# A bank for each pair's small products, and left queries of two batches in one stage: linear attention and a maxout feed-forward on one core

## The chip, the cores and the metric

The kernel runs on one core of one Trainium2 chip. The metric is the device time of one execution in microseconds (us). Before the change the median of 3 runs is 717.27 us (717.15 to 717.32). Engines are named as the profile names them: PE (matmul), PEld (weight load of PE), DVE (vector), ACT (scalar), POOL and SP (whose queue issues the DMAs).

## The reference

Softmax over features for the queries, over positions for the keys, a linear attention, and then a maxout feed-forward on the rows of all heads side by side:

```python
batch, n_heads, seq, head_dim = (8, 8, 576, 64)
q_s = exp(q - max(q, -1)); q_s = q_s / (sum(q_s, -1) + 1e-09)
k_s = exp(k - max(k, 2));  k_s = k_s / (sum(k_s, 2) + 1e-09)
kv = np.einsum('bhsd,bhse->bhde', k_s, v)
attn = np.einsum('bhsd,bhde->bhse', q_s, kv)
x = attn.transpose(0, 2, 1, 3).reshape(4608, 512)
h = maximum(maximum(x @ w1, x @ w2), x @ w3)      # 512 -> 768
out = h @ w_out                                   # 768 -> 512
```

Queries, keys, values and the output are fp32, the weights fp64 in memory. The 576 positions of a batch are handled as 512 "main" rows and 64 "left" rows.

## The kernel before, in words

**Pairs.** Two heads of one batch are a pair (class `Pair`, L374); there are 8 x 4 = 32 of them, numbered n = 4b + g. A pair makes a 128x128 block-diagonal matrix of its two `kv` (L503 to L538, "bd"), and then its 128 rows of the transposed x: 512 main columns and 64 left columns (`x_steps`, L650). The pairs of batches 0 and 1 are "turned": keys and queries are loaded by rows and transposed on PE (L441, L464, L636; the left rows at L445, L466, L640). The query's exps are ten small ACT operations of 128x64 with their sums (L567) for the pairs in `Q_BY_ACT`, and a DVE or POOL subtraction, one exp and a DVE sum for the others (L572, L587, L589). The pairs of later batches use other paths (L475, L580 to L623) and start only when the step "turn" (L818) is reached: all weight slices are split, and all left products of batch 1 are there.

**Weights.** The weights lie in memory as fp64 and come in 24 slices of 512x128 or 128x512 (class `Slice`), each loaded by one DMA of 512 KB and split by ACT, DVE and POOL into a high and a low fp32r part (L342 to L370).

**Chunks.** A chunk is the 512 main rows of one batch; chunk 8 is the 64 left rows of all eight batches (the tile `left`). For each of 18 gates (3 weights x 6 column blocks) PE runs four groups of three fp32r matmuls (L693), one group for each pair's x; then ACT and DVE form the maximum (L702 to L712), and a second product (L732) makes the output.

**PSUM.** There are eight banks: four for the accumulators of gates and output (pool `pf`), three for pairs (`pa`), and one bank `ps` whose four quarters are handed out in turn to every small product: the left transposes of k (`kTl`), of its exps (`kel`) and of q (`qTl`), the `kv` product, and the left x product (L305, L306).

**Order of the work.** Nothing is ordered by the code's sequence. Every operation is a `Step` with a planned cost, its inputs, its rooms (buffers) and a rank. `Streams.run` (L142) simulates all engines and issues the step that can begin first; among those that can, the lowest rank goes first. The order of each engine's instructions that comes out is fixed in the program. The constants in L34 to L43 set the ranks: `AT` for the pairs of the first two batches, `FIRST` and `CHUNK` for the later ones, `SLICES_AT` and what follows for the weights, `GATES_AT` for the gates, and `FIRST_LOADS` for the first DMAs. The rooms in L302 limit what the planner may have open at once; `pf` is a queue whose order is written out beforehand (`in_pf`).

Of the kernel before, what the change touches and what calls it, by code (L numbers as in the profile page):

```python
# [42 lines left out]
Q_BY_ACT = (0, 1, 2, 3, 4, 5, 6)  # L43
# [36 lines left out]
class Streams:  # L80
# [115 lines left out]
def linear_attention_then_maxout_ffn(  # L196
# [26 lines left out]
    nc = tc.nc  # L223
# [22 lines left out]
    pa = ctx.enter_context(tc.tile_pool(name="pa", bufs=3, space=PSUM))  # L246
    ps = ctx.enter_context(tc.tile_pool(name="ps", bufs=1, space=PSUM))
# [16 lines left out]
    q0 = early.tile([P, H, 5, D], F32, name="q0")  # L264
    v0 = early.tile([P, H, 5, D], F32, name="v0")
    bdf = [start.tile([P, P], F32, name=f"bdf{i}", bufs=1) for i in range(2)]
    qbuf = [start.tile([P, 2, 5, D], F32, name=f"q1{i}", bufs=1) for i in range(2)]
# [14 lines left out]
    nc.gpsimd.memset(q0[LEFT:P, :, 4, :], 0.0)  # L282
    for i in range(2):
        nc.gpsimd.memset(bdf[i], 0.0)
    for i in range(2):
        nc.gpsimd.memset(qbuf[i][LEFT:P, :, 4, :], 0.0)
        nc.gpsimd.memset(vbuf[i][:, :, :, D:NV], 1.0)
        nc.gpsimd.memset(vbuf[i][LEFT:P, :, 4, :], 0.0)
# [13 lines left out]
    st = Streams({"pf": 4, "pa": 3, "ps": 4, "keT": 1, "hp": NJ, "tmp": 3, "ke": 2, "qe": 2, "qf": 1, "qt": 2, "tb": 1, "qT": 2, "qhl": 1}, {"pf": in_pf})  # L302
# [71 lines left out]
    class Pair:  # L374


        def __init__(self, b, g):
# [7 lines left out]
            else:  # L385
                self.kt, self.vt = kbuf[self.m], vbuf[self.m]
                if self.turned:
                    self.kt = self.kt.rearrange("p h s d -> p (h s d)").rearrange("p (s h d) -> p s h d", s=5, h=2)

        def ago(self, what, *u):  # L390

            return (what, self.n - 2, *u) if self.n >= 2 else None

# [15 lines left out]
        def v_load(self):  # L409
            if self.b:  # L410
                prev = self.ago("kv") if self.n >= NP + 2 else None
                for hh in range(2):
                    yield Step("S", 0.64, [prev], kb=200)
# [4 lines left out]
        def q_load(self):  # L418
            if self.b == 0:
                return  # L420
            if self.turned:
                prev = self.ago("qsub") if self.n >= NP + 2 else None
                self.qt = qbuf[self.m]
                yield Step("S", 0.64, [prev], kb=256)
                nc.sync.dma_start(out=self.qt[:, :, 0:4, :], in_=main_rows(q, self.b, self.hs))
                yield Step("S", 0.64, gives=("q", self.n), kb=50)
                nc.sync.dma_start(out=self.qt[0:LEFT, :, 4, :], in_=left_rows(q, self.b, self.hs))
# [6 lines left out]
        def k_turned(self):  # L434

            n, kt = self.n, self.kt
            rooms = [("pa", ("kT", n)), ("ps", ("kTl", n))]
            yield Step("T", 0.6, [("k", n)], take=rooms + [("keT", n)], gives=("ksub", n))
            kT = pa.tile([P, CH], F32, name="pa")
            for s in range(4):  # L440
# [3 lines left out]
            kTl = next(small)  # L444
            nc.tensor.transpose(  # L445
                out=kTl[:, :LEFT], in_=kt[:LEFT, 4].rearrange("p h d -> p (h d)"), identity=ident[:LEFT, :LEFT]
            )
            yield Step("V", dve_reduce(CH) + dve_reduce(LEFT) + 0.13)
            km = att.tile([P, 2], F32, name="km2", bufs=4)
            nc.vector.tensor_reduce(out=km[:, 0:1], in_=kT, op=ALU.max, axis=AX.X, negate=True)  # L450
            nc.vector.tensor_reduce(out=km[:, 1:2], in_=kTl[:, :LEFT], op=ALU.max, axis=AX.X, negate=True)
            nc.vector.tensor_tensor(out=km[:, 0:1], in0=km[:, 0:1], in1=km[:, 1:2], op=ALU.min)
            yield Step("A", act(CH) + act(LEFT) + 0.2, free=rooms)
            keT = start.tile([P, S], F32, name="keT", bufs=1)
            ks = self.ks = att.tile([P, 2], F32, name="ks", bufs=4)
            nc.scalar.activation(out=keT[:, :CH], in_=kT, func=AF.Exp, bias=km[:, 0:1], accum_out=ks[:, 0:1])  # L456
            nc.scalar.activation(
                out=keT[:, CH:], in_=kTl[:, :LEFT], func=AF.Exp, bias=km[:, 0:1], accum_out=ks[:, 1:2]
            )
            rooms = [("pa", ("ke", n)), ("ps", ("kel", n))]  # L460
            yield Step("T", 0.6, take=rooms + [("ke", n)], free=[("keT", n)])
            kep = pa.tile([P, CH], F32, name="pa")
            for s in range(4):
                nc.tensor.transpose(out=kep[:, s * P : (s + 1) * P], in_=keT[:, s * P : (s + 1) * P], identity=ident)  # L464
            kel = next(small)
            nc.tensor.transpose(out=kel[:LEFT, :], in_=keT[:, CH:], identity=ident)  # L466
            e = yield Step("AV", (act(CH) + act(P), dve(CH) + dve(P)), free=rooms)
            ke = self.ke = att.tile([P, 5, 2, D], F32, name="ke")
            for o, i in (
                (ke[:, 0:4].rearrange("p s h d -> p (s h d)"), kep),  # L470
                (ke[:LEFT, 4].rearrange("p h d -> p (h d)"), kel[:LEFT, :]),
            ):
                (nc.scalar.copy if e == "A" else nc.vector.tensor_copy)(out=o, in_=i)
# [24 lines left out]
        def k_steps(self):  # L498
# [3 lines left out]
            last = [("ps", ("kv", n))]  # L502
            yield Step(  # L503
                "T", 0.9, [("v", n), self.ago("xmm", 0), self.ago("xmm", 1)], take=last, free=[("ke", n)], gives=("kv", n)
            )
            kv = next(small)
# [17 lines left out]
            yield Step("A", 0.65, free=last if turned else (), gives=("bd", n) if turned else None)  # L524
            for r in heads:
                to = (bdf if turned else bdh)[self.m]
                nc.scalar.activation(out=to[r, r], in_=kv[r, 0:D], func=AF.Copy, scale=rk[r])
            if not turned:
                yield Step("V", 0.45, free=last, gives=("bd", n))
# [11 lines left out]
        def q_steps(self):  # L541
            n = self.n
            rows = 10 if self.turned else QS
            by_act = n in Q_BY_ACT
            qm = att.tile([P, rows], F32, name=f"qm{rows}", bufs=4)
            qs = att.tile([P, rows], F32, name=f"qs{rows}", bufs=4)
            yield Step("V", dve_reduce(rows * D), [("q", n)])
            if self.turned:
# [4 lines left out]
                if by_act:  # L553
                    yield Step("A", 5 * 0.33, take=[("qe", n)])
# [4 lines left out]
                qe = self.qe = start.tile([P, 5, 2, D], F32, name="qe", bufs=2)  # L559
                rows3 = qe.rearrange("p s h d -> p (s h) d")  # L560
                sums = qs.rearrange("p (s h) -> p s h", h=2)
                if by_act:
                    for hh in range(2):
                        if hh:
                            yield Step("A", 5 * 0.33, gives=("qsub", n))
                        for s in range(5):
                            nc.scalar.activation(  # L567
                                out=qe[:, s, hh, :], in_=src[:, hh, s, :], func=AF.Exp,
                                bias=qm[:, 5 * hh + s : 5 * hh + s + 1], accum_out=sums[:, s, hh : hh + 1],
                            )  # L570
                else:
# [3 lines left out]
                        in1=qm.rearrange("p (h s) -> p h s", h=2).unsqueeze(3).broadcast_to([P, 2, 5, D]),  # L575
                        op=ALU.subtract,
                    )
            else:
# [5 lines left out]
                )  # L584
            if not by_act:
# [4 lines left out]
            yield Step("V", 0.34)  # L590
# [39 lines left out]
        def turned_steps(self):  # L630

            n = self.n
            yield Step("T", 0.5, [("qn", n)], take=[("qf", n), ("pa", ("qT", n)), ("ps", ("qTl", n))], free=[("qe", n)])
            qT = pa.tile([P, CH], F32, name="pa")
            for s in range(4):
# [3 lines left out]
            qTl = next(small)  # L639
            nc.tensor.transpose(  # L640
                out=qTl[:, :LEFT], in_=self.qe[:LEFT, 4].rearrange("p h d -> p (h d)"), identity=ident[:LEFT, :LEFT]
            )
            e = yield Step("AV", (act(CH), dve(CH)), free=[("pa", ("qT", n))])
            qf = start.tile([P, S], F32, name="qf", bufs=1)
            (nc.scalar.copy if e == "A" else nc.vector.tensor_copy)(out=qf[:, :CH], in_=qT)
            yield Step("A", act(LEFT), free=[("ps", ("qTl", n))], gives=("qhl", n))
            nc.scalar.copy(out=qf[:, CH:], in_=qTl[:, :LEFT])
            self.terms = [(bdf[self.m], qf)]

        def x_steps(self, u):  # L650
# [3 lines left out]
            room = ("ps" if u else "pa", ("x", u, n))  # L654
            cost = f32(w) if self.turned else 3 * f32r(w)
# [3 lines left out]
            yield Step("T", cost, after, take=[room], gives=("xmm", n, u), free=[("qf" if self.turned else "qhl", n)] if u else ())  # L659
            xT = (next(small) if u else pa.tile([P, CH], F32, name="pa"))[:, :w]  # L660
            last = len(self.terms) - 1
            for i, (l, r) in enumerate(self.terms):
                nc.tensor.matmul(out=xT, lhsT=l, rhs=r[:, cs], start=(i == 0), stop=(i == last))  # L663
# [4 lines left out]
            nc.vector.tensor_sub(out=lo, in0=xT, in1=h.bitcast(F32))  # L668

    class Chunk:
# [124 lines left out]
    def landed(g):  # L797
        for ch in "kqv":
            yield Step("-", 0.0, [("%smain" % ch, g), (ch.upper(), min(g, 1))], gives=(ch, g))
# [5 lines left out]
    def open_late():  # L805
        yield Step("-", 0.0, [(x, 0, g) for x in ("x", "xl") for g in range(NP)], gives="late")
# [11 lines left out]
    def open_turn():  # L818
        yield Step("-", 0.0, [("split", n) for n in range(NS)] + [("xl", 1, g) for g in range(NP)], gives="turn")
        start_stack.close()  # L820
        turn_pools.append(ctx.enter_context(tc.tile_pool(name="turn", bufs=1, side="right", reuse_waits="tile")))
        for i in range(2):
            nc.gpsimd.memset(kbuf[i][LEFT:P, :, 4, :], LOWEST)
        for name, to in (("bdh", bdh), ("bdl", bdl)):
# [39 lines left out]
    for (b, g), p in pairs.items():  # L864
# [14 lines left out]
        for u in range(2):  # L879
# [44 lines left out]
```

## Time and profile before

| | |
|---|---|
| profiled execution, its own time | 717.27 us |
| its span, first to last instruction | 715.5 us |
| PE busy | 685.4 us (96%) |
| DVE, ACT, POOL busy | 401.7, 254.0, 55.1 us |
| first matmul of PE | 8.43 us |
| first matmul of a gate (L693) | 33.11 us |
| granted TensorE clock, mean | 0.998 |

Matmuls are pipelined and their ends are modelled, so the 391 ns of one fp32r matmul of 512 columns are not what it adds: 12 of them in a row took 2.73 us in the chain of waits, 0.23 us each. The time lost by PE is read from its idle time (with what ended it) and from the column of the granted clock.

### The profile page before, as it was taken

What the parts mean: (1) busy time and instruction counts of PE and PEld (TensorE: products, weight loads), DVE (VectorE), ACT (ScalarE), POOL (GpSimd) and SP (SyncE); (2) the same over time, 40 slices, a digit from 0 to 9 for tenths busy, and PEclk for the clock granted to TensorE, in tenths of its full rate; (3) what the DMA queues carried; (4) which work ended last, traced back from release to release, by engine and by line L of the source; (5) the groups of instructions that cost most, each with busy time, mean ns of one, the idle gap of its engine ahead of it and who ended that gap; (6) DMA issues with size and microseconds to landing.
All of it is one profiled execution on the core that took longest, in us unless ns stands there. A gap on an engine that the chain in (4) does not pass through costs nothing.

```text
span 715.5 us, 9842 instructions
## 1 busy us (share of the span) xinstructions
PE 685.4 (96%) x3528; PEld 552.0 (77%) x3528; DVE 401.7 (56%) x812; ACT 254.0 (36%) x605; POOL 55.1 (8%) x69
## 2 busy tenths in 40 slices
PE   3779899999999999999999999999999999999997
PEld 2457687787888787888888888888888888888885
DVE  6789867388977977865477646653422112211220
ACT  4899745433443425422442234223411111111111
POOL 1222233100010000000000000000000000000000
PEclk9999999999999999999999999999999999999999
DMA  8947423315454334520253015200200010010002
GB/s 222 252 135 231 127 83 106 109 34 129 113 163 122 83 80 110 151 65 17 73 150 86 16 49 164 64 16 28 82 1 0 16 45 0 1 44 16 1 0 60
DMA packets 86417, 58.07 MB, mean 81 GB/s; under 512 B 53344, under 2 KB 77920, under 8 KB 86368
## 3 DMA queue, kind: packets, MB, share of 16 engines
q1 hardware_dynamic: 86288, 57.31, 28.9%
q8 instruction: 28, 0.46, 0.3%
q14 instruction: 21, 0.17, 0.1%
q10 hardware_dynamic: 80, 0.13, 0.0%
HBM read 40.89 MB, written 9.44 MB: 70 GB/s over the span
## 4 chain that ended last, share of the span: by engine, by line
PE 88%; ACT 4%; DVE 4%; DMA 2%; issue 1%; SPq 1%; DVEq 0%; ACTq 0%
PE pf L693 59%; PE pf L732 21%; PE ps L511 3%; PE pa L663 2%; ACT qe L567 2%; PE ps L663 1%; DMA wst<-in_moe_w_dram 1%; ACT keT L456 1%; ACT wst L359 0%; PE pa L464 0%; DMA v<-in_v_dram 0%; DVE m L705 0%; DVE wx L346 0%; PE pa L441 0%; DMA vt<-in_v_dram 0%
## 5 line engine op out<-in xcount | busy, mean ns | idle before, releaser
L693 PE MATMUL pf<-x,wh 128*128 128x512 f32 x1152 | 357.3, 391 | 0.0
L693 PEld LDWEIGHTS pf<-x,wh 128*128 128x128 f32 x1152 | 217.3, 189 | 47.0 <-issue 1.0
L693 PE MATMUL pf<-x,wl 128*128 128x512 f32 x576 | 231.1, 401 | 0.0
L705 DVE TENSOR_TENSOR m<-pf,m 128x512 f32<-128x512 f32 x108 | 74.4, 689 | 180.0 <-PE pf L693 177.5
L693 PEld LDWEIGHTS pf<-x,wl 128*128 128x128 f32 x576 | 108.7, 189 | 23.9 <-issue 0.7
L708 ACT CAST h_h<-m 128x512 fp32r<-128x512 f32 x54 | 33.6, 622 | 191.6 <-DVE m L705 191.4
L732 PE MATMUL pf<-ol,h_h 128*128 128x512 f32 x216 | 88.0, 408 | 0.1
L732 PE MATMUL pf<-oh,h_l 128*128 128x512 f32 x216 | 84.5, 391 | 0.0
L732 PE MATMUL pf<-oh,h_h 128*128 128x512 f32 x216 | 84.3, 390 | 0.0
L702 ACT COPY m<-pf 128x512 f32<-128x512 f32 x54 | 31.7, 587 | 57.8 <-PE pf L693 57.7
L732 PEld LDWEIGHTS pf<-ol,h_h 128*128 128x128 f32 x216 | 40.6, 188 | 9.2 <-DVE ol L370 0.7
L712 DVE TENSOR_TENSOR h_l<-m,h_h 128x512 fp32r<-128x512 f32 x54 | 36.9, 683 | 19.1 <-ACT h_h L708 19.0
L732 PEld LDWEIGHTS pf<-oh,h_l 128*128 128x128 f32 x216 | 40.5, 188 | 9.1
L732 PEld LDWEIGHTS pf<-oh,h_h 128*128 128x128 f32 x216 | 40.6, 188 | 7.6
L693 PE MATMUL pf<-left,wh 128*128 128x512 f32 x144 | 44.4, 389 | 0.0
L486 POOL PARTITION_ALL_REDUCE kma<-km x24 | 18.7, 779 | 299.7 <-DVE ke L489 146.8
L750 ACT COPY m<-pf 128x512 f32<-128x512 f32 x35 | 20.4, 587 | 59.8 <-PE pf L732 54.3
L355 POOL TENSOR_TENSOR wst<-wx,wst 128x512 int32<-128x512 int32 x24 | 31.6, 1318 | 90.9 <-DVE wx L351 55.5
L668 DVE TENSOR_TENSOR x<-pa,x 128x512 fp32r<-128x512 f32 x32 | 22.1, 689 | 29.4 <-ACT x L666 29.3
L600 DVE STREAM_TRANSPOSE tb<-qt 128x576 f32<-128x576 f32 x24 | 30.8, 1282 | 2.4 <-DMA qT<-tb 2.1
L666 ACT CAST x<-pa 128x512 fp32r<-128x512 f32 x32 | 18.7, 585 | 36.1 <-PE pa L663 36.1
L693 PEld LDWEIGHTS pf<-left,wh 128*128 128x128 f32 x144 | 27.0, 188 | 5.7
(114 smaller groups left out, 679.2 us busy)
## 6 DMA issues: line engine op xcount, KB each, us to landing
wst<-in_moe_w_dram SPq DMA_DIRECT2D x18, 512.0 KB, 5.0
out_dram<-m SPq DMA_DIRECT2D x32, 256.0 KB, 2.4
vt<-in_v_dram SPq DMA_DIRECT2D x56, 128.0 KB, 3.0
qt<-in_q_dram SPq DMA_DIRECT2D x24, 288.0 KB, 3.1
qT<-tb SPq DMA_DIRECT2D x192, 36.0 KB, 1.9
kt<-in_k_dram SPq DMA_DIRECT2D x24, 256.0 KB, 3.0
wst<-in_moe_w_out_dram SPq DMA_DIRECT2D x6, 512.0 KB, 3.3
q<-in_q_dram SPq DMA_DIRECT2D x8, 256.0 KB, 4.6
```

The costliest lines, as they stand in the source:

```text
L355: nc.gpsimd.tensor_add(out=low.bitcast(I32), in0=x.bitcast(I32), in1=low.bitcast(I32))
L511: nc.tensor.matmul(out=kv[r, :nv], lhsT=ke[rows, s, hh, :], rhs=self.vt[rows, hh, s, 0:nv], start=(s == 0), stop=(s == 4),)
L600: nc.vector.transpose(out=tb.rearrange("p e (c s) -> p s e c", s=QS), in_=self.qt.rearrange("p s (e c) -> p s e c", e=2))
L663: nc.tensor.matmul(out=xT, lhsT=l, rhs=r[:, cs], start=(i == 0), stop=(i == last))
L668: nc.vector.tensor_sub(out=lo, in0=xT, in1=h.bitcast(F32))
L693: nc.tensor.matmul(out=ps, lhsT=l[:, cc, js], rhs=r, start=(cc == 0 and t == 0), stop=(cc == NC - 1 and t == 2))
L702: nc.scalar.copy(out=m, in_=self.m.pop((j, 0)))
L705: nc.vector.tensor_max(out=m, in0=self.m.pop((j, i)), in1=m)
L708: nc.scalar.copy(out=h, in_=m)
L712: unit[e].tensor_sub(out=lo, in0=m, in1=h.bitcast(F32))
L732: nc.tensor.matmul(out=po, lhsT=l, rhs=r[:, j, :], start=(j == 0 and i == 0), stop=(j == NJ - 1 and i == 2))
L750: nc.scalar.copy(out=o, in_=po)
```

## The change: what it does

- **Banks.** The bank `ps` and its quarters are gone. Each pair takes one tile of a whole bank (`take_small`), whose quarters hold that pair's `kTl` and later its left x product, its `kel`, its `kv`, and sums of queries. For the pairs of batch 0 this tile is one of the four `pf` banks, ahead of the gates in that pool's queue; for all other pairs it comes from a pool `sm` of one bank. A turned pair holds it from its k transposes until its block-diagonal matrix is made; a later pair holds it from `kv` until its left x product has been read. That left product is still a step of its own after the main one.
- **Left queries.** The turned pairs no longer load, exponentiate, transpose or multiply their 64 left query rows: their query tiles are 4 blocks instead of 5, the exps of a pair 8 instead of 10. A new stage `left_queries` does it once for batches 0 and 1 (64 rows of each in 128 partitions, all 8 heads), after "turn". The step "turn" waits for main x products of batch 1 instead of the left ones, "late" for those of batch 0 alone; the gates of chunk 8 wait for the new stage.
- **Pair 1** is in `Q_AFTER`: its queries are exponentiated without sums, multiplied unnormalized, and divided afterwards; the sums come from a small product with `of_head`, and x is transposed by PE.
- **Query exps.** `Q_BY_ACT` is (0, 3, 4, 5, 6, 7) instead of (0, ..., 6).
- **Storage.** Every turned pair has its own block-diagonal matrix (`bdf`, 8 of them); v of batch 1 lies compactly; ones and zeros in the v tiles are set at "turn".
- **Ranks.** All constants of the order are others, the first loads have another order (without left queries), the gates' rank lies behind that of all pairs, and the planner counts PE steps before 34 us at 1.85 times their cost.

```diff
+COLD = 34.0, 1.85
-FIRST, CHUNK, SLICE = 21.0, 39.5, 0.35
-AT = (16.0, 6.9, 25.7, 26.2, 99.1, 87.2, 114.2, 74.5)
-STEP = (0.38, 3.02)
-SLICES_AT, SLICE_STEP, SLICE_HI, SLICE_LO = -30.5, 2.83, 6.78, 0.26
-GATES_AT = 50.0
-FIRST_LOADS = 'qwQKkKqvVvwQkkwqVkwqvv'
+FIRST, CHUNK, SLICE = 143.0, 39.5, 1.32
+AT = (38.7, -49.7, 32.6, 13.7, 143.7, 146.4, 163.0, 85.8)
+STEP = (7.87, 0.38)
+SLICES_AT, SLICE_STEP, SLICE_HI, SLICE_LO = -59.7, 0.11, 1.39, 0.51
+GATES_AT = 1000.0
+FIRST_LOADS = 'vkwkKqvwKVwVqqkwvqkv'
+BANKS = 3, 1
-Q_BY_ACT = (0, 1, 2, 3, 4, 5, 6)
+Q_BY_ACT = (0, 3, 4, 5, 6, 7)
+Q_AFTER = (1,)
...
+        if e == "T" and t < COLD[0]:
+            c *= COLD[1]
...
-    ps = ctx.enter_context(tc.tile_pool(name="ps", bufs=1, space=PSUM))
+    sm = ctx.enter_context(tc.tile_pool(name="sm", bufs=BANKS[1], space=PSUM))
...
-    in_pf = []
+    in_pf = [("sm", n) for n in range(NP)]
...
-    quarters = ps.tile([P, 4, P], F32, name="ps")
-    small = (quarters[:, i % 4, :] for i in itertools.count())
...
+        def small_room(self):
+            return ("pf", ("sm", self.n)) if self.b == 0 else ("sm", self.n)
+        def take_small(self):
+            self.sm = (pf if self.b == 0 else sm).tile([P, CH], F32, name="pf" if self.b == 0 else "sm")
...
-            kv = next(small)
+            if not turned:
+                self.take_small()
+            kv = self.sm[:, 2 * P : 3 * P]
...
-            yield Step("A", 0.65, free=last if turned else (), gives=("bd", n) if turned else None)
+            yield Step("A", 0.65, free=[self.small_room()] if turned and not after else (), gives=("bd", n) if turned else None)
...
+            if self.after:
+                yield Step("A", act(rows * D), gives=("qn", n))
+                nc.scalar.activation(out=rows3, in_=rows3, func=AF.Exp)
+                return
...
+            xn, sums = pa.tile([P, CH], F32, name="pa"), self.sm[:, 3 * P : 4 * P]
+            for s in range(4):
+                l = qf[:, s * P : (s + 1) * P]
+                nc.tensor.matmul(out=sums[:, 2 * s : 2 * s + 2], lhsT=l, rhs=of_head, start=True, stop=True)
+                nc.tensor.matmul(out=xn[:, s * P : (s + 1) * P], lhsT=l, rhs=bdf[:, n], start=True, stop=True)
...
+            yield Step("V", dve(CH), take=[("qe", ("xn", n))], free=room, gives=("qhl", n))
+            xr = self.xr = start.tile([P, 8, D], F32, name="qe", bufs=2)
+            nc.vector.tensor_tensor(
+                out=xr, in0=xn.rearrange("p (r d) -> p r d", d=D), in1=qs.unsqueeze(2).broadcast_to([P, 8, D]), op=ALU.mult
+            )
...
-            xT = (next(small) if u else pa.tile([P, CH], F32, name="pa"))[:, :w]
+            xT = self.sm[:, 0:LEFT] if u else pa.tile([P, CH], F32, name="pa")
+            if after_sums:
+                for s in range(4):
+                    nc.tensor.transpose(...)
...
+    def left_queries():
+        yield Step("S", 0.64, ["turn"], take=[("qt", "left")], kb=128)
...
+        nc.sync.dma_start(out=ql[0:LEFT], in_=left_rows(q, 0, slice(0, H)))
+        nc.sync.dma_start(out=ql[LEFT:P], in_=left_rows(q, 1, slice(0, H)))
...
+        nc.vector.tensor_reduce(out=qm, in_=ql, op=ALU.max, axis=AX.X)
+        nc.vector.tensor_tensor(out=ql, in0=ql, in1=qm.unsqueeze(2).broadcast_to([P, H, D]), op=ALU.subtract)
+        nc.scalar.activation(out=ql, in_=ql, func=AF.Exp)
+        nc.vector.tensor_reduce(out=qs, in_=ql, op=ALU.add, axis=AX.X)
...
+        nc.vector.tensor_tensor(out=ql, in0=ql, in1=qs.unsqueeze(2).broadcast_to([P, H, D]), op=ALU.mult)
+        for g in range(NP):
+            nc.tensor.transpose(
+                out=qTp[:, g * P : (g + 1) * P], in_=ql[:, 2 * g : 2 * g + 2].rearrange("p r d -> p (r d)"), identity=ident
+            )
+        nc.scalar.copy(out=qT[:, :CH], in_=qTp)
+        for n in range(TURNED * NP):
+            b, g = divmod(n, NP)
+            at = g * P + b * LEFT
+            nc.tensor.matmul(out=xT[:, at : at + LEFT], lhsT=bdf[:, n], rhs=qT[:, at : at + LEFT], start=True, stop=True)
+        nc.scalar.copy(out=h, in_=xv)
+        nc.vector.tensor_sub(out=lo, in0=xv, in1=h.bitcast(F32))
...
-                x = [("x", c, cc)] if c < B else [("xl", b, cc) for b in range(B)]
+                x = [("x", c, cc)] if c < B else ["left", *(("xl", b, cc) for b in range(TURNED, B))]
...
-        yield Step("-", 0.0, [(x, 0, g) for x in ("x", "xl") for g in range(NP)], gives="late")
+        yield Step("-", 0.0, [("x", 0, g) for g in range(NP)], gives="late")
...
-        yield Step("-", 0.0, [("split", n) for n in range(NS)] + [("xl", 1, g) for g in range(NP)], gives="turn")
+        yield Step("-", 0.0, [("split", n) for n in range(NS)] + [("x", 1, g) for g in range(NP)], gives="turn")
...
+    st.add(left_queries(), FIRST + CHUNK * 4)
```

More of the change, by code (lines that the diff above doesn't have):

```diff
@@ L281, in linear_attention_then_maxout_ffn @@
         )
[L282 to L288, printed above, removed]
+    nc.gpsimd.memset(of_head, 0.0)
+    for h, r in enumerate(heads):
+        nc.gpsimd.memset(of_head[r, h : h + 1], 1.0)
+    nc.gpsimd.memset(bdf, 0.0)
     def main_rows(src, b, hs):
@@ L455, in k_turned @@
             ks = self.ks = att.tile([P, 2], F32, name="ks", bufs=4)
             nc.scalar.activation(out=keT[:, :CH], in_=kT, func=AF.Exp, bias=km[:, 0:1], accum_out=ks[:, 0:1])
[L457 to L462, printed above, removed]
+            nc.scalar.activation(out=keT[:, CH:], in_=kTl, func=AF.Exp, bias=km[:, 0:1], accum_out=ks[:, 1:2])
@@ L463, in k_turned @@
+            room = [("pa", ("ke", n))]
+            yield Step("T", 0.6, take=[*room, ("ke", n)], free=[("keT", n)])
+            kep, kel = pa.tile([P, CH], F32, name="pa"), self.sm[:LEFT, P : 2 * P]
             for s in range(4):
                 nc.tensor.transpose(out=kep[:, s * P : (s + 1) * P], in_=keT[:, s * P : (s + 1) * P], identity=ident)
-            kel = next(small)
-            nc.tensor.transpose(out=kel[:LEFT, :], in_=keT[:, CH:], identity=ident)
-            e = yield Step("AV", (act(CH) + act(P), dve(CH) + dve(P)), free=rooms)
+            nc.tensor.transpose(out=kel, in_=keT[:, CH:], identity=ident)
@@ L468, in k_turned @@
+            e = yield Step("AV", (act(CH) + act(P), dve(CH) + dve(P)), free=room)
             ke = self.ke = att.tile([P, 5, 2, D], F32, name="ke")
[L469 to L473, printed above, removed]
+            copy = nc.scalar.copy if e == "A" else nc.vector.tensor_copy
@@ L475, in k_plain @@
+            copy(out=ke[:, 0:4].rearrange("p s h d -> p (s h d)"), in_=kep)
+            copy(out=ke[:LEFT, 4].rearrange("p h d -> p (h d)"), in_=kel)
         def k_plain(self):
@@ L501, in k_steps @@
             ke = self.ke
-            last = [("ps", ("kv", n))]
+            after = turned and n in Q_AFTER
             yield Step(
-                "T", 0.9, [("v", n), self.ago("xmm", 0), self.ago("xmm", 1)], take=last, free=[("ke", n)], gives=("kv", n)
-            )
-            kv = next(small)
+                "T", 0.9, [("v", n), *([] if turned else [self.ago("xmm", u) for u in range(2) if n - 2 >= TURNED * NP or u == 0])], take=() if turned else [self.small_room()],
+                free=[("ke", n)], gives=("kv", n),
+            )
+            if not turned:
+                self.take_small()
+            kv = self.sm[:, 2 * P : 3 * P]
             nv = D if turned else NV
@@ L542, in q_steps @@
             n = self.n
-            rows = 10 if self.turned else QS
+            rows = 8 if self.turned else QS
             by_act = n in Q_BY_ACT
+            self.after = self.turned and n in Q_AFTER
             qm = att.tile([P, rows], F32, name=f"qm{rows}", bufs=4)
@@ L638, in turned_steps @@
                 )
-            qTl = next(small)
-            nc.tensor.transpose(
-                out=qTl[:, :LEFT], in_=self.qe[:LEFT, 4].rearrange("p h d -> p (h d)"), identity=ident[:LEFT, :LEFT]
-            )
[L643 to L648, printed above, removed]
+            e = yield Step("AV", (act(CH), dve(CH)), free=room, gives=None if self.after else ("qhl", n))
+            (nc.scalar.copy if e == "A" else nc.vector.tensor_copy)(out=qf, in_=qT)
+            if not self.after:
+                self.terms = [(bdf[:, n], qf)]
+                return
+            room = [("pa", ("xn", n))]
+            yield Step("T", 1.2, [("bd", n)], take=room, free=[("qf", n)])
+            xn, sums = pa.tile([P, CH], F32, name="pa"), self.sm[:, 3 * P : 4 * P]
[3 more added lines that the diff above has]
+                nc.tensor.matmul(out=xn[:, s * P : (s + 1) * P], lhsT=l, rhs=bdf[:, n], start=True, stop=True)
+            yield Step("V", 0.45, free=[self.small_room()])
+            qs = att.tile([P, 8], F32, name="qs8", bufs=4)
+            nc.vector.tensor_scalar_add(out=qs, in0=sums[:, 0:8], scalar1=1e-9)
+            nc.vector.reciprocal(out=qs, in_=qs)
+            yield Step("V", dve(CH), take=[("qe", ("xn", n))], free=room, gives=("qhl", n))
+            xr = self.xr = start.tile([P, 8, D], F32, name="qe", bufs=2)
+            nc.vector.tensor_tensor(
+                out=xr, in0=xn.rearrange("p (r d) -> p r d", d=D), in1=qs.unsqueeze(2).broadcast_to([P, 8, D]), op=ALU.mult
+            )
         def x_steps(self, u):
@@ L658, in x_steps @@
                 after += [("gates", b - 2) if b >= 2 else None, "late" if b == 1 else None]
-            yield Step("T", cost, after, take=[room], gives=("xmm", n, u), free=[("qf" if self.turned else "qhl", n)] if u else ())
-            xT = (next(small) if u else pa.tile([P, CH], F32, name="pa"))[:, :w]
-            last = len(self.terms) - 1
-            for i, (l, r) in enumerate(self.terms):
-                nc.tensor.matmul(out=xT, lhsT=l, rhs=r[:, cs], start=(i == 0), stop=(i == last))
+            yield Step("T", cost, after, take=[] if u else [room], gives=("xmm", n, u), free=[freed] if u or self.turned else ())
+            xT = self.sm[:, 0:LEFT] if u else pa.tile([P, CH], F32, name="pa")
+            if after_sums:
+                for s in range(4):
+                    nc.tensor.transpose(
+                        out=xT[:, s * P : (s + 1) * P], in_=self.xr[:, 2 * s : 2 * s + 2].rearrange("p r d -> p (r d)"),
+                        identity=ident,
+                    )
+            else:
+                last = len(self.terms) - 1
+                for i, (l, r) in enumerate(self.terms):
+                    nc.tensor.matmul(out=xT, lhsT=l, rhs=r[:, cs], start=(i == 0), stop=(i == last))
             h, lo = self.x_place(u)
```

97 lines of the change are left out of this document (64 added, 33 removed).

## The prediction, made before the changed kernel ran

> **What bounds the kernel now.** I read the page first, for the busy time of the engines.
>
> ```profile
> span 715.5 us, 9842 instructions
> ## 1 busy us (share of the span) xinstructions
> PE 685.4 (96%) x3528; PEld 552.0 (77%) x3528; DVE 401.7 (56%) x812; ACT 254.0 (36%) x605; POOL 55.1 (8%) x69
> ```
>
> PE is idle for 30.1 us of the span. The other engines count only where they make PE wait, so the question is where those 30.1 us lie. The busy time by stretches answers it; the columns are the length, then busy time (and instructions) of PE, PEld, DVE, ACT and POOL, the granted clock, the DMA share and GB/s. I cut the stretches at PE's own events.
>
> ```profile
> 8.43:20.00 11.57, 7.78 (x41) 5.24 (x42) 8.75 (x20) 8.71 (x36) 2.56 (x2) 1.00 1.03 238
> 20.00:33.11 13.11, 7.95 (x45) 5.42 (x43) 9.75 (x23) 10.88 (x53) 2.58 (x2) 1.00 1.08 272
> 33.11:47.97 14.86, 13.19 (x90) 9.62 (x88) 12.80 (x30) 13.18 (x50) 3.28 (x3) 1.00 0.41 120
> 47.97:59.64 11.67, 8.40 (x59) 5.96 (x55) 10.30 (x28) 11.32 (x44) 3.22 (x3) 1.00 0.53 169
> 59.64:73.39 13.75, 13.75 (x65) 11.32 (x62) 12.61 (x29) 11.43 (x32) 2.64 (x2) 1.00 0.94 279
> 73.39:82.36 8.97, 6.73 (x50) 4.40 (x49) 8.75 (x19) 6.72 (x23) 3.10 (x3) 0.91 0.28 73
> ```
>
> Idle PE time in the six: 3.79, 5.16, 1.67, 3.27, 0 and 2.24, together 16.1 us; with 8.43 us before the first matmul that is 24.6 of the 30.1. From 82.36 us PE has practically no gap, so the change can gain only before that point (or by less PE work), and can lose anywhere. From 33.11 to 59.64 ACT is busy 24.50 of 26.53 us and DVE 23.10: that stage belongs to those two. Next, the waits of PE alone (total, times, longest):
>
> ```profile
> PE pa L441 <- DMA k<-in_k_dram: 8.4, 1, 8.4
> PE pa L464 <- ACT keT L456: 2.5, 1, 2.5
> PE ps L511 <- DVE km L451: 2.5, 2, 1.5
> PE pa L636 <- DVE qe L595: 1.8, 2, 0.9
> PE ps L663 <- ACT keT L457: 1.6, 1, 1.6
> PE ps L640 <- ACT keT L457: 1.4, 1, 1.4
> PE ps L511 <- ACT keT L457: 1.4, 1, 1.4
> PE ps L511 <- ACT ke L473: 1.2, 1, 1.2
> PE ps L640 <- DVE left L668: 1.2, 1, 1.2
> PE ps L511 <- ACT qf L647: 1.0, 1, 1.0
> ```
>
> `kv` (L511) has no use for a maximum (L451) or a copy of queries (L647), nor the left product (L663) for an exp of keys (L457). These are other pairs' quarters of the one bank `ps`: 2.5 + 1.6 + 1.4 + 1.4 + 1.2 + 1.0 = 9.1 us of waits for a reader of another quarter. The planner counts four rooms there and does not know of them. Only the L464, L636 and L511-on-L473 rows are real inputs. Last, PE's timeline at three places (start, length, instruction, idle time before it):
>
> ```profile
> 44.56 0.60 PE L441 MATMUL pa<-ident,kt 128*128 128x128 f32 x4
> ```
> ```profile
> 55.05 1.02 PE L663 MATMUL pa<-qf,bdf 128*128 128x512 f32 x2
> ```
> ```profile
> 77.32 0.43 PE L663 MATMUL ps<-qf,bdf 128*128 128x64 f32 x2 [0.63 <-DVE km L451]
> 79.14 0.95 PE L511 MATMUL ps<-vt,ke 128*64 128x64 f32 x20 [1.38 <-ACT keT L457]
> ```
> ```profile
> 81.07 1.06 PE L441 MATMUL pa<-ident,kt 128*128 128x128 f32 x4
> ```
> ```profile
> 81.00:82.00 1.00, 1.00 (x5) 0.73 (x4) 1.00 (x3) 1.00 (x7) 0.16 (x1) 0.50 0.58 132
> ```
>
> The product at 55.05 is the last main x of batch 0: no gate can be finished before it. The 2.2 us of waits from 73 to 82 are all on the bank, and behind them the clock falls to 0.50: the same four transposes take 1.06 us instead of 0.60. By the stretch's mean clock of 0.91, and the half second after it, this costs 1.7 us (3.4 us at half speed).
>
> **The change, part by part.** The sum is made against the profiled execution's own 717.27 us, which is also the median of the three runs shown; its span of 715.5 leaves 1.8 us around it that I hold fixed. A difference under 0.2% (1.4 us) cannot be told from none here.
>
> *Work of PE.* Eight left transposes of queries go, and four of 128x128 come; the eight left products move to the new stage in the same number.
>
> ```profile
> L640 PE MATMUL ps<-ident,qe 64*128 64x64 f32 x8 | 2.4, 296 | 2.6 <-ACT keT L457 1.4 <-DVE left L668 1.2
> ```
> ```profile
> L636 PE MATMUL pa<-ident,qe 128*128 128x128 f32 x32 | 5.8, 313 | 1.8 <-DVE qe L595 1.8
> ```
>
> That is -2.4 + 4 x 0.18 (5.8/32) = -1.7 us. Pair 1 adds four transposes (0.7) and four two-column products, between 0 and 0.3 us each by the L640 row; its normalizing product has the columns of the one it replaces. Middle: -1.7 + 0.7 + 0.6 = **-0.4 us** (bounds -1.7 and +0.9).
>
> *The way to the last x of batch 0.* Fewer query exps on ACT:
>
> ```profile
> L567 ACT ACTIVATE qe<-q,qm 128x64 f32<-128x64 f32 x70 | 23.4, 341 | 0.2
> ```
> ```profile
> L587 ACT ACTIVATE qe<-qe 128x640 f32<-128x640 f32 x1 | 0.7, 738 | 2.1 <-DVE qe L572 2.1
> ```
> ```profile
> L666 ACT CAST left<-ps 128x64 fp32r<-128x64 f32 x32 | 6.8, 214 | 17.3 <-PE ps L663 13.7 <-DVE wx L347 2.2 <-PE ps L511 1.4
> ```
>
> Batch 0 has 40 small exps now and 16 afterwards: 24 x 0.341 = 8.2 us less, two whole exps of at most 0.738 more, and two left copies fewer for each of four pairs, 8 x 0.214 = 1.7. Together 8.4 us less on an engine with 2.0 us free in the stage. DVE gets three operations more (two subtractions, one sum) and loses four small ones:
>
> ```profile
> L550 DVE TENSOR_REDUCE qm<-q 128x10 f32<-128x640 f32 x8 | 6.4, 809 | 0.0
> ```
>
> 3 x 0.81 = +2.4 us at most. So DVE, with 3.4 us free from 33.11 to 59.64, is late next, and ACT's 8.4 us aren't passed on whole. The other ranks put batch 1's pairs behind batch 0's, which takes some DVE work out of the stage. I take the last x 5 us earlier (bounds 0 and 8.4). Against it stand the banks: before that x four accumulators hold three groups each; the last pair of batch 0 holds one of the four until its matrix is made, so three groups come later. A group's price:
>
> ```profile
> 212.01 2.73 PE pf L693 x12
> ```
>
> 12 matmuls are four groups, 0.68 us each; three are 2.0 us. In all **-3.0 us** (bounds -8.4 and +2.0). The bank waits before 59.64 are inside this term.
>
> *73 to 82 us.* The 2.2 us of waits have no counterpart with a bank for each pair, since within a pair the small products follow one another anyway; the half clock (1.7 us) goes with the gap. At most -3.9; since real inputs of the same pairs may be late next, **-3.0 us** (bounds -3.9 and 0).
> The Trainium skill ("TensorE: Matmul & The Clock Gate", "What's actually happening") has the clock fall after an idle window of about 3.4 us. Here the longest wait before the fall was 1.38 us, so the trace goes further than the rule; by the rule the half clock would not hang on these waits, and this term would be -1.7 instead of -3.0.
>
> *The rest* I cost at nothing. The new stage's DVE, ACT and PE steps come after "turn" and are first read by chunk 8's gates; hundreds of us of gates cover them. Its two DMAs replace six on SP; SP is in order, and if their buffer is late the loads of later pairs queue behind them. The v tiles' constants move to POOL at "turn", ahead of pair 8's loads:
>
> ```profile
> L288 POOL MEMSET vt<- 64x130 f32 x2 | 0.5, 230 | 0.1
> ```
>
> This is under 1 us with the ones. What covers the late stages is one margin, from the chain of waits and the stretch in which batch 2 is prepared:
>
> ```profile
> 203.81 0.70 PE pa L663 x3
> ```
> ```profile
> 143.47:212.01 68.54, 68.54 (x400) 55.11 (x400) 59.23 (x128) 27.98 (x54) 6.73 (x8) 1.00 0.40 106
> ```
>
> The last x of batch 2 starts at 203.81, and its gates at 212.01. With 0.7 us for the product, 0.6 for the copy and 0.7 for the subtraction, the margin is 6.2 us. DVE paces these pairs (59.23 of 68.54 us), and they begin at "turn". If "turn" stays where it is, a gain up to 6.2 us passes untouched, and more than that turns into a wait here.
>
> Sum: -0.4 - 3.0 - 3.0 = -6.4 us; 717.27 - 6.4 = **710.9 us**. Late next would be DVE, at the last x of batch 0 and at batch 2.
>
> **The rivals.**
> 1. *More.* ACT's 8.4 us pass on whole, the planned order costs no bank, and 73 to 82 gives 3.9: -0.4 - 8.4 - 3.9 = -12.7, **704.6 us**. For it: ACT is the fullest engine before 59.64. Against it: DVE's 3.4 us, and the margin of 6.2 us unless "turn" moves too. Chance 0.13.
> 2. *Nothing to measure.* DVE holds the last x where it is, and the bank waits give way to waits for real inputs: -0.4 - 0.4, about **716.5 us** (715 to 718.5). For it: DVE at 23.10 of 26.53 us. Against it: PE idles at bank waits while DVE is behind them in the same bank. Chance 0.16.
> 3. *Slower: the gates find no banks.* In `in_pf` all four small tiles stand ahead of the first gate. If the third and fourth pairs of batch 0 come late, the gates stay shut until the last x: 12 groups x 0.68 = 8.2 us come later instead of 2.0, so +6.2; and PE, with little to do, stays at half speed for some 4 us more, +2: 710.9 + 8.2 = **719.1 us**. It decides if the first gate starts after about 45 us (now 33.11). Chance 0.10.
> The Trainium skill ("Perfetto Trace Analysis", "Optimization Strategy") reads repeated gaps as a sign that PSUM has too few buffers for the next tile; that speaks for this rival, and the gates' three groups per bank before 55.05 agree with it.
> 4. *Slower: "turn" comes late.* One bank `sm` makes batch 1's pairs strictly one after another, behind batch 0 in rank. If the last of them ends 10 us later than now, batch 2's last x is ready at 215.8 while PE arrives at 212.01 - 6.4 = 205.6: **+10.2, 721.1 us**. Against it: four pairs have some 80 us from 60 us on. Chance 0.09.
>
> **How the numbers follow.** Forecast (707 to 714.5): 0.52; the rivals 0.13, 0.16, 0.10, 0.09. The range from 704.5 to 718.5 leaves out the slower rivals and what lies beyond the first, about 2 in 10. Faster by over 0.2%: 0.52 + 0.13 + 0.07 of rival 2 = 0.72; slower 0.19; within 0.2%: 0.09. For the forecast alone the range is 707 to 714.5.
>
> **What would show it.** In the profile after, no PE wait on a small tile should have another pair's reader behind it. The last main x of batch 0 should start near 50 us, PE should have no gap and no half clock from some 55 us on, and ACT should hold far fewer L567 operations before that. The gates of chunk 2 should start near 205.6 us without a wait. A first gate after 45 us, a wait of PE near 200 us, or batch 0's last x still at 55 us would make it wrong.

## The result, and the profile after

The changed kernel takes 712.57 us (median of 6 runs, 710.97 to 715.29), the kernel before 717.3 us in the same comparison (716.95 to 719.56). The ratio is 0.9932, with a 95% interval of 0.9914 to 0.9951: faster by 0.7%. Run again beside the experiments it gave 712.29 us, 0.9933 [0.9915, 0.9951].

The page after, of an execution of 712.87 us:

```profile
span 711.1 us, 9813 instructions
...
## 1 busy us (share of the span) xinstructions
PE 684.1 (96%) x3542; PEld 554.1 (78%) x3542; DVE 400.4 (56%) x804; ACT 250.2 (35%) x554; POOL 57.6 (8%) x71
```

PE is busy 1.3 us less than before and idle for 27.0 us instead of 30.1. The busy time by stretches says where; the columns are length, then busy time of PE, PEld, DVE, ACT and POOL, granted clock, DMA share and GB/s. Before:

```profile
0.00:60.00 60.00, 37.68 (x229) 26.59 (x230) 46.35 (x117) 46.50 (x184) 13.76 (x22) 1.00 0.75 197
60.00:90.00 30.00, 27.76 (x139) 21.70 (x138) 27.16 (x60) 24.70 (x75) 7.82 (x6) 0.94 0.64 188
```

After, and below it three parts of the first stretch:

```profile
0.00:60.00 60.00, 37.91 (x229) 28.64 (x230) 42.58 (x108) 38.93 (x121) 16.27 (x20) 0.86 0.69 186
60.00:90.00 30.00, 29.83 (x156) 23.51 (x154) 26.15 (x56) 25.32 (x74) 9.37 (x8) 1.00 0.66 200
```
```profile
20.00:30.00 10.00, 6.37 (x39) 4.08 (x39) 8.58 (x23) 6.86 (x17) 3.58 (x3) 0.73 0.72 205
30.00:40.00 10.00, 4.91 (x36) 4.60 (x37) 3.64 (x9) 3.79 (x18) 1.29 (x1) 0.67 0.60 174
40.00:50.00 10.00, 9.83 (x57) 6.95 (x56) 8.15 (x21) 8.04 (x19) 2.46 (x2) 0.75 0.49 152
```

From 60 to 90 us PE is full and at full clock: the gaps and the half clock around 80 us have gone. But the first 60 us are no better for PE, although ACT has 7.6 us less to do in them: the half clock now lies between 20 and 50 us, and from 30 to 40 us no engine is half busy. Something outside the engines holds them there. PE's waits after (total, times, longest):

```profile
PE pf L664 <- ACT qf L655: 5.1, 1, 5.1
PE pa L454 <- DMA k<-in_k_dram: 5.1, 1, 5.1
PE pf L457 <- DMA k<-in_k_dram: 3.3, 1, 3.3
PE pa L473 <- ACT keT L467: 3.1, 1, 3.1
PE pa L698 <- ACT bdf L536: 2.6, 1, 2.6
PE pf L520 <- DVE ke L479: 1.0, 1, 1.0
...
PE pf L776 <- ACT bdf L536: 0.7, 1, 0.7
...
PE sm L520 <- DVE left L703: 0.3, 1, 0.3
```

The first six are real inputs of the waiting product. The last two are waits for a bank: a gate for the `pf` bank that the last pair of batch 0 held (0.7 us), and a `kv` product for the reader of another pair's left x in the one bank `sm` (0.3 us). The first wait is the new one. PE's timeline (start, length, instruction, idle time before it):

```profile
36.51 0.59 PE L664 MATMUL pf<-of_head,qf 128*128 128x2 f32 x2 [5.09 <-ACT qf L655]
```
```profile
42.14 0.77 PE L776 MATMUL pf<-x,wl 128*128 128x512 f32 x1
```
```profile
54.48 1.02 PE L698 MATMUL pa<-qf,bdf 128*128 128x512 f32 x2
```

The first gate starts at 42.14 us (33.11 before) and the last main x of batch 0 at 54.48 us (55.05 before). The x is ready when DVE has subtracted its high part. DVE's timeline, before and after:

```profile
57.29 0.69 DVE L668 TENSOR_TENSOR x<-pa,x 128x512 fp32r<-128x512 f32 x1 [0.37 <-ACT x L666]
```
```profile
56.95 0.68 DVE L703 TENSOR_TENSOR x<-pa,x 128x512 fp32r<-128x512 f32 x1
```

These two rows split the gain of the profiled runs, 715.5 - 711.1 = 4.4 us. The *way* to this subtraction became 0.3 us shorter. The *rest* of the span behind it went from 715.5 - 57.29 = 658.2 us to 711.1 - 56.95 = 654.2, 4.0 us shorter. It is idle time that went: behind the subtraction PE is busy 649.4 us before and 649.2 us after. The experiments below are read by the same split. A second profile of the changed kernel (`a0_after`) and of e1 (e12) has the way 0.6 and 0.8 us shorter and the rest at 653.3 and 653.9 us, so differences under 1 us in it say nothing. The gates of chunk 2 start at 207.46 us in the chain of waits (212.01 before), with no wait ahead of them:

```profile
207.46 6.13 PE pf L776 x27
```

### The profile page after: what moved, and what is told of

It reads as the page before. It is cut to its first block, busy times and chain, and to the rows that moved or that the text cites. A ratio compares the mean times of both kernels' runs of the same rounds, so it can differ in the third digit from the quotient of the medians.

```text
span 711.1 us, 9813 instructions
## 1 busy us (share of the span) xinstructions
PE 684.1 (96%) x3542; PEld 554.1 (78%) x3542; DVE 400.4 (56%) x804; ACT 250.2 (35%) x554; POOL 57.6 (8%) x71
## 4 chain that ended last, share of the span: by engine, by line
PE 89%; DMA 4%; DVE 2%; SPq 2%; ACT 1%; issue 0%; DVEq 0%; ACTq 0%
PE pf L776 61%; PE pf L815 21%; DMA wst<-in_moe_w_dram 3%; PE pa L698 3%; PE sm L520 3%; PE sm L698 1%; DMA vt<-in_v_dram 1%; SPq L871 1%; SPq L414 1%; SPq L874 0%; DVE x L703 0%; DVE wl L375 0%; DVE wx L356 0%; PE pa L745 0%; SPq L419 0%
```

## The experiments

Theory 1 after the result: the way would have become some 5 us shorter but for one DMA wait (e1), and the banks of their own made the rest shorter (e2, e5). The rivals: ACT or the first loads set the way in any case, and the rest comes from the new order, not from the banks.

### v of batch 1 as it lay before

SP's timeline of the changed kernel, where the trouble begins, and ACT's at its end:

```profile
22.89 0.64 SPq L428 DMA_DIRECT2D vt<-in_v_dram  x1
27.96 0.63 SPq L430 DMA_DIRECT2D vt<-in_v_dram  x1
...
30.68 0.54 SPq L337 DMA_DIRECT2D wst<-in_moe_w_dram  x1
```
```profile
35.33 0.67 ACT L364 ACTIVATE wst<-wst 128x512 int32<-128x512 uint32 x1 [5.49 <-DMA wst<-in_moe_w_dram]
```

L428 loads the second head of v, L430 the left rows of both heads. 4.4 us pass on SP between the end of the one and the start of the other, and SP's waits name the landing of the DMA just issued:

```profile
SPq L430 <- DMA vt<-in_v_dram: 12.1, 3, 4.7
```

L430 follows L428 into the same tile, though the two write no common element. The slice of weights behind it on SP is issued at 30.68 us, so ACT's split of it (L364), and the copy of queries L655 behind that in ACT's order, come late; PE's L664 waits for that copy. The next pair's L430 waits in the same way, 3.1 us, and the slice behind it comes later still, as ACT's row shows:

```profile
36.63 0.62 SPq L430 DMA_DIRECT2D vt<-in_v_dram  x1
37.35 7.56 SPq L337 DMA_DIRECT2D wst<-in_moe_w_dram  x3
```
```profile
41.25 0.68 ACT L364 ACTIVATE wst<-wst 128x512 int32<-128x512 uint32 x1 [2.13 <-DMA wst<-in_moe_w_dram]
```

The edit leaves the order of every engine's instructions as it is:

```diff
-                    self.vt = self.vt.rearrange("p h s d -> p (h s d)")[:, : 10 * D]
-                    self.vt = self.vt.rearrange("p (h s d) -> p h s d", h=2, s=5)
```

> Only the compact place of v for batch 1 is undone; all engines keep their order. Theory 1 (the DMA of the left rows of v waits for the landing of the head's DMA just before it, and SP, which is in order, holds back the weight slice behind it): SP's gap from 22.9 to 28.0 us goes, the fifth slice lands about 4 to 5 us earlier, PE's wait of 5.1 us before the sums of pair 1 shrinks below 1 us, and the time falls by 3 to 6 us against the changed kernel, to about 708. Rival (the slice is late because the DMA engines are full between 20 and 35 us, whatever SP does): the slice lands at 35 us as before, and the time stays within 1 us.

Measured: 707.79 us, 0.9867 [0.985, 0.9884]; a second time (e12) 707.26 us, 0.9859 [0.9843, 0.9874]. SP, ACT and PE of e1:

```profile
23.18 0.69 SPq L428 DMA_DIRECT2D vt<-in_v_dram  x1
23.92 1.30 SPq L430 DMA_DIRECT2D vt<-in_v_dram  x1
...
27.33 0.54 SPq L337 DMA_DIRECT2D wst<-in_moe_w_dram  x1
```
```profile
29.74 0.63 SPq L430 DMA_DIRECT2D vt<-in_v_dram  x1
30.46 9.50 SPq L337 DMA_DIRECT2D wst<-in_moe_w_dram  x3
```
```profile
31.42 0.68 ACT L364 ACTIVATE wst<-wst 128x512 int32<-128x512 uint32 x1 [1.22 <-DMA wst<-in_moe_w_dram]
```
```profile
36.31 0.67 ACT L364 ACTIVATE wst<-wst 128x512 int32<-128x512 uint32 x1 [1.08 <-DMA wst<-in_moe_w_dram]
```
```profile
32.62 0.39 PE L664 MATMUL pf<-of_head,qf 128*128 128x2 f32 x2 [0.83 <-ACT qf L655]
```
```profile
49.52 1.02 PE L698 MATMUL pa<-qf,bdf 128*128 128x512 f32 x2
```
```profile
51.99 0.69 DVE L703 TENSOR_TENSOR x<-pa,x 128x512 fp32r<-128x512 f32 x1
```

No wait of L430 for a DMA is left. The first slice is issued 3.4 us earlier and L664 starts 3.9 us earlier. The slice behind the second L430 is issued 6.9 us earlier and taken up by ACT 4.9 us earlier; that is the 5.0 us by which the last x starts earlier. The program is 4.5 to 5 us faster. The rest behind the subtraction is 705.7 - 51.99 = 653.7 us, as in the changed kernel. So the whole difference is in the way, and the waits of L430 are its cause; DMA engines that are full whatever SP does, the rival, are not.

> The kernel with strided v once more, beside the three others: 707 to 708.5 us by its first runs, a ratio of 0.985 to 0.988.

The changed kernel in the same comparison as e1:

> The changed kernel as it is, beside the others of this call. From its six runs: 711 to 715.3 us, ratio to before 0.9932. Both theories expect the same here; it shows how far the changed kernel spreads.

712.29 us (711.5 to 715.29). The later experiments start from e1, so that these waits aren't in them.

### The order of before

e1 with the constants of the order, and the order of the first loads, of the kernel before (left queries left out of it; the planner's `COLD` stays):

```diff
-FIRST, CHUNK, SLICE = 143.0, 39.5, 1.32
+FIRST, CHUNK, SLICE = 21.0, 39.5, 0.35
...
-GATES_AT = 1000.0
-FIRST_LOADS = 'vkwkKqvwKVwVqqkwvqkv'
+GATES_AT = 50.0
+FIRST_LOADS = 'qwKkKqvVvwkkwqVkwqvv'
```

> v as in the run before it, and besides all constants of the order as before the change (first loads without the left queries); banks, left stage and pair 1 stay changed. If the banks and the late left stage carry the gain, this is near the run with strided v, 707 to 712 us. If the new order carries it, this is at 715 to 720 us, with PE waits in the first 80 us like those of before.

Measured: 711.59 us, 0.992 [0.9905, 0.9936], in the range for "the banks and the late left stage carry the gain". But that holds for the way alone. The way is shorter still than in e1, but PE has gaps after it:

```profile
50.44 0.69 DVE L703 TENSOR_TENSOR x<-pa,x 128x512 fp32r<-128x512 f32 x1 [0.26 <-ACT x L701]
```
```profile
69.00 1.13 PE L698 MATMUL pa<-qf,bdf 128*128 128x512 f32 x2 [1.15 <-DVE qf L655]
83.43 0.95 PE L520 MATMUL sm<-vt,ke 128*64 128x64 f32 x20 [1.41 <-ACT ke L479]
92.37 0.50 PE L776 MATMUL pf<-x,wl 128*128 128x512 f32 x1 [1.67 <-POOL wl L375]
```

The rest is 709.6 - 50.44 = 659.2 us, not shorter than before's 658.2. With banks of their own the pairs don't wait for each other's readers, but in the old order PE then waits 4.2 us for real inputs. The other corner, the kernel before with the new order (its left queries put next to the main ones in the first loads; no `COLD`):

```diff
-FIRST_LOADS = 'qwQKkKqvVvwQkkwqVkwqvv'
+FIRST_LOADS = 'vkwkKqQvwKVwVqQqkwvqkv'
```

> The kernel before with the new constants of the order (first loads with the left queries put in behind the first and the second q). Theory (order and structure add up: the new order gave 3.8 us on the new structure): 713 to 715 us. Rival (the new order suits only the new structure, since it counts on fewer query steps): 717 us or above.

Measured: 724.12 us, 1.0091 [1.0077, 1.0105], slower than the kernel before. My theory that structure and order simply add up falls; the rival holds. The way is 63.63 us and the rest 721.8 - 63.63 = 658.2.

### One bank for all small products again

e1 with the quarters handed out in turn; the planner knows nothing of it, so every engine's order stays:

```diff
+    quarters = sm.tile([P, 4, P], F32, name="sm")
+    small = (quarters[:, i % 4, :] for i in itertools.count())
...
-            kv = self.sm[:, 2 * P : 3 * P]
+            kv = next(small)
```

(likewise for `kTl`, `kel`, the sums and the left x product)

> The kernel with strided v; every engine keeps its order, and the planner still counts a bank for each pair, but all small products are taken in turn from the quarters of one bank, as before the change. If waits for readers of another pair's quarter are a cost by themselves (theory 1), PE waits at small products come back, some 4 to 9 us of them before 80 us, and the time rises by 3 to 6 us over the run with strided v, to 711 to 714. Rival (they only stood in for other waits): within 1.5 us of the run with strided v.

Measured: 708.33 us, 0.9876 [0.9859, 0.9894], which can't be told from e1. Theory 1, which wanted 3 us or more, falls. PE's waits show that the bank's waits are indeed back:

```profile
PE sm L520 <- DVE km L463: 1.8, 2, 1.5
...
PE sm L664 <- ACT qf L655: 1.8, 1, 1.8
PE sm L457 <- ACT ke L479: 1.3, 2, 0.6
```

but they lie ahead of the last x: the subtraction starts at 53.67 us, 1.7 us later than in e1, of which the median shows 0.5. The stretch that was to profit from the banks is full without them:

```profile
60.00:90.00 30.00, 30.00 (x171) 23.88 (x170) 27.70 (x58) 24.89 (x69) 8.51 (x7) 1.00 0.59 175
```

The same edit on e2, the old order:

> The kernel with the order's old constants and strided v (711.6 us), every engine in the same order, but all small products in the quarters of one bank again. Under the new order the shared bank cost only 0.5 us. Theory 2 (shared quarters cost only where several turned pairs are under way at once, as in the old order): 3 to 5 us slower, 714.5 to 716.5. Rival (the bank hardly matters in any order, and the left queries and the spread of the exps carry the gain of 6 us): within 1 us of 711.6.

Measured: 714.93 us, 0.996 [0.9947, 0.9972], beside 0.992 [0.9905, 0.9936] for e2: here the shared bank costs some 3 us. The subtraction moves from 50.44 to 52.82 us, and the rest stays (712.0 - 52.82 = 659.2). So the banks act on the way, not on the rest, and their worth depends on the order.

### Two banks for small products of later pairs

```diff
-BANKS = 3, 1
+BANKS = 2, 2
```

> v strided; two banks for the small products of later pairs and two instead of three for the large ones. If the single small bank holds up the pairs of batch 1 and of the later batches, this is faster than the run with strided v by 1 us or more. If the large products need their three banks more, or PE has no gap after 55 us to lose, it is the same or up to 4 us slower.

Measured: 709.82 us, 0.9892 [0.9874, 0.991], 2.0 us more than e1. A second bank `sm` isn't worth the third large one here, and e1 has no wait of PE on `sm` over 0.2 us that it could take away. (The planner makes another order of it, with the subtraction at 58.75 us and less work of PE left behind it, so its way and rest can't be set beside e1's.)

### Pair 1 and the query exps

e1 with pair 1 made like the others of batch 0 (`Q_AFTER = ()`):

> v strided; pair 1 on the ordinary way (subtraction, one exp, a sum on DVE, and its x by one product), planned anew. Theory 1 (the way of pair 1 is worth little, the banks and the order carry the gain): within 2 us of the run with strided v, either way. Rival (dividing late takes pair 1 off the busy DVE and ACT in the stage that sets the last x): 3 us or more slower, 711 or above.

Measured: 710.67 us, 0.9905 [0.9892, 0.9919]; the subtraction starts at 55.27 us. It is 2.9 us more than e1, between the two expectations. e1 with pair 1 plain and the exps of pairs 0 to 6 on ACT, as before:

```diff
-Q_BY_ACT = (0, 3, 4, 5, 6, 7)
+Q_BY_ACT = (0, 1, 2, 3, 4, 5, 6)
-Q_AFTER = (1,)
+Q_AFTER = ()
```

> v strided; the query exps as before the change (pairs 0 to 6 by small exps on ACT, pair 7 not, pair 1 on the ordinary way), planned anew. Theory (fewer small exps on ACT before the last x of batch 0 are worth some us): 710.7 us or more, that is slower than pair 1 alone on the ordinary way. Rival (ACT has room there by now): 707 to 710.

Measured: 710.48 us, 0.9899 [0.9886, 0.9913], the same as e4, and again between the two expectations. Between the two kernels lie 16 small exps of batch 0 on ACT, and they change nothing that can be measured. Pair 1's other way is worth some 3 us. Both kernels were planned anew, so a new order of the engines is in these figures too.

### The last early slice of weights, later

The fourth slice of weights among e1's first loads, last of all:

```diff
-FIRST_LOADS = 'vkwkKqvwKVwVqqkwvqkv'
+FIRST_LOADS = 'vkwkKqvwKVwVqqkvqkvw'
```

> v strided; of the first loads the fourth weight slice comes last instead of before v of pair 2, so that keys and values of pairs 2 and 3 do not queue behind it, planned anew. If the landing of the last pair's keys sets the last x of batch 0, that x starts 2 to 4 us earlier than at 49.5 us and the time falls by 1 to 3 us. If the slices or DVE set it, the time stays within 1 us or grows by up to 3 us since a slice is later.

Measured: 716.89 us, 0.9993 [0.9981, 1.0004]: all of e1's gain is gone. The last x product starts at 53.12 us, but its copy and subtraction are planned late, and PE waits for both:

```profile
57.34 0.80 PE L776 MATMUL pf<-x,wl 128*128 128x512 f32 x1 [2.32 <-ACT x L701]
59.60 1.22 PE L776 MATMUL pf<-x,wh 128*128 128x512 f32 x2 [1.46 <-DVE x L703]
```

It is another order on all engines, so it shows how much hangs on the order, not what one load is worth.

### A warm clock in the first stage

e1 with 48 transposes of the identity, whose results nobody reads, ahead of PE's steps in the first 25 us:

```diff
+        def spin(self, k): [nc.tensor.transpose(out=idle[:, 0:P], in_=ident, identity=ident) for _ in range(k)]
...
+            self.spin(20 if n == 1 else 0); yield Step("V", 0.35)
```

> v strided; 48 transposes whose result nobody reads are put into four stretches in which PE waits (before the first keys, twice behind them, and after kv of pair 1), so that the clock comes up early and stays up. Theory 1 (PE's half-speed steps lie on the way to the last x): the clock is full from about 10 us, and the time falls by 2 to 5 us. Rival (ACT, DVE and the loads set the last x, PE's steps are short beside them): the clock is full as well, but the time stays within 1 us.

Measured: 707.96 us, 0.9869 [0.9853, 0.9884], the same as e1. The dummies ran until 26.5 us, yet the clock fell behind them (stretches, then PE's timeline):

```profile
30.00:40.00 10.00, 8.05 (x49) 7.12 (x50) 6.58 (x19) 7.46 (x27) 1.28 (x1) 0.60 0.66 196
```
```profile
23.28 3.26 PE L401 MATMUL sm<-ident 128*128 128x128 f32 x20
30.12 0.95 PE L520 MATMUL pf<-v,ke 128*64 128x64 f32 x20 [1.74 <-ACT ke L479]
32.89 0.59 PE L664 MATMUL pf<-of_head,qf 128*128 128x2 f32 x2 [1.83 <-ACT qf L655]
```

e1 had 0.92 in this stretch, without the dummies. So the clock wasn't full, and what a full one would bring isn't tested. What the lower one cost can be read at the next product that needs ACT's exps, L473. It follows in e1, in e12 (0.80 in this stretch) and in e8:

```profile
39.88 0.65 PE L473 MATMUL pa<-ident,keT 128*128 128x128 f32 x4 [2.59 <-ACT keT L467]
```
```profile
39.11 0.66 PE L473 MATMUL pa<-ident,keT 128*128 128x128 f32 x4 [0.93 <-ACT keT L467]
```
```profile
41.23 1.05 PE L473 MATMUL pa<-ident,keT 128*128 128x128 f32 x4
```

In e1 and e12 PE waits here for ACT: a slower PE ahead of this point uses up its wait, and a faster one would only wait longer. In e8 the wait is gone, and the last x product starts at 50.81 us, 1.3 us later than in e1. That profile is of the longest of e8's four executions (708.42 us); the medians don't show the difference. So ACT sets the last x in e1, and PE has about 2.6 us to spare.

### All of them in the split

Profiled span, start of the subtraction for the last x of batch 0, the rest, and PE's idle time in the rest. e2, e11, e4, e10, e3 and e7 were planned anew:

| kernel | structure, order | span | way | rest | idle in it |
|---|---|---|---|---|---|
| before | old, old | 715.5 | 57.29 | 658.2 | 8.8 |
| e11 | old, new | 721.8 | 63.63 | 658.2 | 9.9 |
| e9 | new with one bank, old | 712.0 | 52.82 | 659.2 | 9.5 |
| e2 | new, old | 709.6 | 50.44 | 659.2 | 8.7 |
| after | new with compact v, new | 711.1 | 56.95 | 654.2 | 4.9 |
| e5 | new with one bank, new | 706.5 | 53.67 | 652.8 | 4.5 |
| e1 | new, new | 705.7 | 51.99 | 653.7 | 4.6 |
| e4 | e1, pair 1 plain | 708.9 | 55.27 | 653.6 | 5.6 |
| e10 | e1, exps and pair 1 as before | 708.0 | 55.02 | 653.0 | 5.9 |
| e8 | e1, dummies | 706.6 | 53.14 | 653.5 | 4.4 |
| e3 | e1, two small banks | 708.0 | 58.75 | 649.3 | 4.8 |
| e7 | e1, fourth slice last | 715.9 | 58.85 | 657.1 | 6.3 |

The idle time tells two groups apart: 8.7 to 9.9 us where the structure or the order is old, 4.4 to 6.3 where both are new; some 4.5 us of it lie at the end of every kernel. The rest follows it (658 to 659 us and 653 to 654), but for e3 and e7, where the plan also moved work of PE across the split. So the shorter rest needs both the new structure and the new order. Within the new structure the bank for each pair has no part in it (e5), and neither has pair 1's way (e4) or the spread of the exps (e10), each taken alone. What is left, the late left queries above all, wasn't tried by itself. The way differs with nearly everything that was changed.

## Why the prediction was right in its number and wrong in a step

The forecast was 710.9 us, the result 712.57: inside the range, on the side that had the most chance. But two misses of opposite sign lie under it, and that they partly cancel is luck.

1. **Work of PE, -0.4.** Busy time fell by 1.3 us, within its bounds (the half clock is in it as well).
2. **The way to the last x, -3.0.** In the changed kernel it is worth 0.3 us: the x product starts at 54.48 us, not near 50. The step that failed is "the rest I cost at nothing". I counted SP's DMAs, and named what queues behind one, but looked only at the new stage's own; that the new place of v could make one load wait for another wasn't considered. It cost 4.5 to 5 us of the program. Without it the x starts at 49.52 us, as the prediction had it, and the term is 57.29 - 51.99 = 5.3 us.
3. **Its cause.** I derived it from ACT's fewer small exps. e10 against e4 shows nothing for them, in the two orders that the planner made. What the experiments can assign is pair 1's other way (3 us) and, in the old order, the banks (3 us). What leaving out the left queries brings alone wasn't tried; it stays open how much of the remainder it is.
4. **73 to 82 us, -3.0.** The size was right: the rest is 4.0 us shorter, there are no gaps and no half clock. The reason was wrong. I gave it to the bank for each pair; in e2 the banks are there and the rest isn't shorter, because the waits for real inputs (4.2 us) take their place, just as my second rival had it; in e5 they aren't there and it is shorter. That its size came near is therefore luck. It is the new order with the new structure.
5. **Rival 3** (gates without banks, decided by a first gate after about 45 us) came close: 42.14 us in the changed kernel, because of the DMA waits; 35.66 in e1. **Rival 4** was absent: chunk 2's gates began at 207.46 us without a wait, and a second bank `sm` at the price of a large one (e3) made it slower.
6. **The left stage and the v constants at nothing.** No wait of PE for the new stage or for the v constants shows in the profile after, so nothing speaks against it. The one row that names `left` (0.3 us) is the bank wait above.

Without the DMA waits the change is worth some 10 us. e1 is the best version of all: faster than before by 1.3 to 1.4%, and than the change by 4.5 us.

What stays open: why the left rows' DMA waits for the second head's in the compact v and not in the strided one. In the compact tile the left rows of the two heads lie in columns 256 to 319 and 576 to 639, and the second head's main rows in 320 to 575, between them. But the strided tile, with 65 columns for a block instead of 64, is interleaved in the same way, so that alone doesn't tell the two apart.

## What to carry to other kernels

When a diff moves a buffer's layout, list for every DMA into it which semaphores it waits for: two loads that share no element can still be put one behind the other, and on an in-order queue all that follows pays. A wait that is seen on a shared buffer is worth what remains when the next input becomes the limit; try the buffer under both orders before giving it the gain. And split the span at the event that the later work hangs on: a sum that comes out right can hide two misses.

## What the runs showed of the hardware

The granted clock fell without a long gap. In e8 no wait of PE between 10 and 40 us was longer than 1.83 us, and the clock was 0.60 from 30 to 40 us. The Trainium skill ("TensorE: Matmul & The Clock Gate", "What's actually happening") ties the fall to an idle window of about 3.4 us; this trace shows a fall with about half of that, so the gaps alone don't tell it.

PE at this lower clock cost no time as long as it used up a wait for ACT: of 2.59 us in e1, 0.93 were left in e12, and the last x came no later. In e8 nothing was left, and it came 1.3 us later than in e1. A DMA of one head's v took 4.4 us from the end of its issue to the release of the one that waited for it; by two such waits in a row (4.4 and 3.1 us) a weight slice was issued 6.9 us later than in e1, and ACT, which waits 1.08 us for it in e1, took it up 4.9 us later.
